# Another written order of matmuls in the attention quads that also hold an output piece

## The chip, the cores and the metric

One core of a Trainium2 chip runs the whole program. The metric is device time in microseconds of one execution. Engines are named as in the profile: PE is TensorE (PEld its weight loads), DVE VectorE, ACT ScalarE, POOL GpSimd, and SP the engine that issues nearly all DMAs.

## What is computed

A block of attention with one key and value head for 32 query heads, and a two-layer GELU network, each behind layer norms and scaled by rows made from a condition vector `c`. There are 2048 tokens of 576 numbers, heads of 18, and 4608 hidden numbers. The core of the reference:

```
mod = (silu(c) @ w_mod).reshape(6, 576)          # sa, ca, ga, sb, cb, gb
h = layernorm(x) * (1 + ca) + sa
q = (h @ wq) in 32 heads of 18;  k = h @ wk;  v = h @ wv
p = softmax(q k^T * 18 ** -0.5)                  # over 2048 keys, for each head
x = x + ga * (concat over heads (p v) @ wo)
h = layernorm(x) * (1 + cb) + sb
x = x + gb * (gelu(layernorm(h) @ w1 + b1) @ w2 + b2)
```

## The kernel before

**Stages.** The first makes keys, values and queries. The second is the attention, about 1230 us of the span, and the change lies in it. The third is the two-layer network.

**Quads.** The attention goes over 32 quads: a block of 512 tokens (`tb`, four of them) and four heads (`qd`, eight of them). A quad has, for 16 chunks of 128 keys (`kc`):

- Scores, `st_mm` (line 927): 64 matmuls of 64 x 128 by 64 x 512 (line 931) into psB banks. ACT takes the exp of each into a tile P (line 933). P has four buffers, each with four exps.
- Products, `pv_mm` (line 914): P times V (line 921), four matmuls side by side in columns, into the one psC bank. They run eight groups (`LAG`) behind the exps, that is two tiles P.
- Maxima for the next quad (some units for the one after), `mx_mm` (line 937): 48 score matmuls (line 319) into psM banks, each reduced by DVE (line 953). For eight units one more pair is folded: an X matmul (line 941, psB) is copied by ACT with a Relu into one of two buffers `xc` (line 944), and the R matmul (line 319, psM) is then reduced with it by DVE's custom operation (line 951).
- F1 and F2: `smax_fin1` reduces the maxima of quad n+1 to a column (lines 352 and 353, DVE, tile `mxf`), `smax_fin2` transposes it on PE (line 357, psB), negates it on ACT (line 359) and splits off its remainder on DVE (line 360). Four DMAs (line 364) write it as rows into the query tile QST of quad n+1, whose scores can't start before.
- The end of the quad before, `post_quad` (line 733): ACT copies psC to O when its last product is done (line 738). T1 transposes O on DVE (line 741), RC takes the reciprocal (line 744) and has POOL scale (line 745), T2 transposes back (line 747), OS copies on ACT (line 757) and subtracts on POOL (line 758), and four DMAs store the pair.
- Between tiles, `between` (line 955) lets other work step on: query loads, the second layer norm, and the weight preparation on POOL.

Score and maximum matmuls use half of PE's rows each: group 0 the lower 64, group 1 the upper.

**Buffers.** psB has four banks, psM three, psC one. A matmul that takes a bank waits until the engine that reads that bank has read its use before.

**The written order.** Engines work in order, so the order in which the program emits instructions is the order of each engine. The loop from line 980 reads it from a list of tokens, one list for each kind of quad. `S0` and `S1` are the next score of group 0 or 1, `M0`, `M1` the next maximum matmul, `X1`, `R1` the folded pair, `V4`, `V3`, `V2` as many quarters of 128 columns of the next products, `WO` an output piece, and the rest as above. `QUAD` (line 884) serves quads 0 to 8. `QUADW` (line 889) serves quads 9 to 30 and holds one `WO`, 64 `S`, 48 `M`, 8 `X1`, 8 `R1` and V tokens of 64 quarters in all; quad 31 has a list of its own.

**The output piece.** `wo_next` (line 970) takes half a tile's columns of the output product: 14 matmuls into one psB bank (line 723) and an addition on DVE (line 727). In the quads where a tile of the second layer norm is ready for it, five transposes (line 155) follow at once, in two psB banks, copied by ACT (line 165) and DVE (line 167). The same norm has its statistics on DVE (lines 143, 147, 148), which step on in `between`, at the end of every second tile of products. They come to a pattern of two quads: quads with one parity (here called even) hold statistics near F1 and the transposes at WO, the odd ones statistics near T1 and T2. From quad 27 on there are none.

Of the kernel before, what the change touches and what calls it, by code (L numbers as in the profile page):

```python
# [32 lines left out]
def block_kernel(ctx: ExitStack, tc, x, wqkv, wo, w1, b1, w2, b2, c, wmod, ident_in, out):  # L33
# [460 lines left out]
    WO, YR, ATT, B2 = {}, {}, {}, {}  # L494
# [374 lines left out]
    def tail_parts(o, tail, d, e=po):  # L869

        e.tensor_tensor(d, tail[:, 0], tail[:, 1], op=ALU.subtract)
        for x, y in ((o[:, :2], tail), (o[:, 2], d)):
# [13 lines left out]
            M1 V3 M0 S1 S1 M0 S0 R1 S0 V3 R1 S0 S1 M1 S0 M0 X1 V3 M0 S1 M0 S1 S0 S0 R1 V3 M0 X1 S0 M1 S0 M1  # L886
            V3 S1 M0 M0 S1 T2 S0 S1 V4 M0 S1 S0 M1 S0 M1 V3 S0 R1 S1 M0 F1 S1 S0 V3 X1 M0 S1 M0 R1 S0 F2 OS
            V4 M0 M1 S0 S1 M0 X1 V4 S1 M0 S1 S0 M1 M0 S1 V2 R1 S0 M1 S0 V2 S0 S1 M0 M1 V2 S1""".split()
    QUADW = """S0 M1 S0 S1 M0 S1 V4 M0 S1 M0 S1 S0 M1 V4 X1 M0 M1 S0 T1 X1 S0 V4 S0 M1 M0 S1 M0 S1 V4 S1 S0 RC
            R1 M0 S1 S0 R1 V4 S1 M0 S1 S0 M0 X1 M0 V3 S0 M1 S1 M0 S1 M0 S1 V3 S0 M1 S0 X1 M0 T2 OS V2 M0 R1  # L890
            S0 S1 S0 M1 WO X1 M0 S1 M0 R1 S0 V4 S1 M0 S1 M0 S1 M0 S1 V3 M1 S0 S0 M1 S0 S1 M0 V3 S0 M1 R1 S0
            S1 M0 V3 S0 M1 M1 S0 X1 S0 V3 M1 M0 S0 S1 R1 S0 V4 M0 S1 M0 F1 S0 S1 M0 S1 V4 F2 S1 M0 X1 M0 S1
            M0 V2 S1 S0 M1 S0 V2 M1 S0 S1 M0 V2 M0 S1 M0 S1 S1 S0 M1 V3 M0 X1 S0 R1 S0 R1 V3""".split()
    LASTW = "S0 S1 S0 S1 S0 S1 WO V4 S0 S1 V4".split()
    LAST = "S0 S1 S0 S1 V4 S0 S1 S0 S1 V4".split()
    P, PVt = {}, {}
# [83 lines left out]
    for n in range(NQT):  # L980
        ns = [0, 0]
        if n < NQT - 1:
            order = QUADW if n > NQ else QUAD
            if n == NQT - 2:
# [520 lines left out]
```

## Time and profile before

| what | value |
|---|---|
| median of 3 runs | 2234.67 us (2234.5 to 2235.53) |
| profiled execution | 2233.75 us |
| its span, first to last instruction | 2232.0 us |
| mean granted clock of PE | 0.998 |
| attention, quads 0 to 31 | about 128 to 1360 us of the span |
| quads 9 to 30 (`QUADW`) | about 469 to 1344 us |

Rows of the timeline begin with the start and the duration of a group of instructions, then the engine, the line, the operation, its output and inputs, and how many there are. A bracket behind them tells how long the engine stood idle before the group and what released it. Starts can be compared between engines. PE's matmuls are pipelined and their ends are modelled, so on PE the reader should take differences of starts, not durations. A row of the waits names the waiting engine, tile and line, what it waited for, and then the total in us, the times and the longest. A row of the windows gives the bounds of a stretch and its length, then the busy time and instructions of PE, PEld, DVE, ACT and POOL, the granted clock, the DMA share and GB/s.

### The profile page before, as it was taken

What the parts mean: (1) busy time and instruction counts of PE and PEld (TensorE: products, weight loads), DVE (VectorE), ACT (ScalarE), POOL (GpSimd) and SP (SyncE); (2) the same over time, 40 slices, a digit from 0 to 9 for tenths busy, and PEclk for the clock granted to TensorE, in tenths of its full rate; (3) what the DMA queues carried; (4) which work ended last, traced back from release to release, by engine and by line L of the source; (5) the groups of instructions that cost most, each with busy time, mean ns of one, the idle gap of its engine ahead of it and who ended that gap; (6) DMA issues with size and microseconds to landing.
All of it is one profiled execution on the core that took longest, in us unless ns stands there. A gap on an engine that the chain in (4) does not pass through costs nothing.

```text
span 2232.0 us, 45861 instructions
## 1 busy us (share of the span) xinstructions
PE 2206.7 (99%) x16454; PEld 1437.8 (64%) x16454; DVE 1936.0 (87%) x3415; ACT 1645.7 (74%) x3145; POOL 1529.3 (69%) x1761
## 2 busy tenths in 40 slices
PE   7999999999999999999999999999999999999999
PEld 5654444444444445444454445888888898988898
DVE  7589999999999999999999982887888878888887
ACT  5579999999999999999999997444444544343443
POOL 6653456777877787778776200888888867877776
PEclk9999999999999999999999999999999999999999
DMA  6232143443433333333333101655665646676563
GB/s 232 84 129 92 34 138 121 150 135 116 145 118 123 124 135 112 124 132 121 129 124 128 44 13 60 200 179 176 180 179 175 189 126 182 182 216 189 177 185 123
DMA packets 184776, 307.99 MB, mean 138 GB/s; under 512 B 19711, under 2 KB 75407, under 8 KB 184549
## 3 DMA queue, kind: packets, MB, share of 16 engines
q1 hardware_dynamic: 184405, 304.91, 43.0%
q8 instruction: 130, 2.13, 0.4%
q14 instruction: 97, 0.79, 0.1%
q10 hardware_dynamic: 144, 0.15, 0.0%
HBM read 200.97 MB, written 93.79 MB: 132 GB/s over the span
## 4 chain that ended last, share of the span: by engine, by line
PE 88%; DVE 3%; ACT 3%; issue 1%; POOL 0%; ACTq 0%; POOLq 0%; DVEq 0%
PE psC L921 22%; PE psB L1144 18%; PE psA L1247 16%; PE psB L931 14%; PE psM L319 11%; PE psB L723 2%; ACT P L933 2%; PE psB L941 2%; PE psA L1281 1%; DVE mx L953 1%; PE psA L723 1%; DVE xc L951 1%; PE psB L155 0%; PE psB L357 0%; PE psB L248 0%
## 5 line engine op out<-in xcount | busy, mean ns | idle before, releaser
L933 ACT ACTIVATE P<-psB 128x512 f32<-128x512 f32 x2008 | 1043.6, 617 | 32.3 <-PE psM L319 10.4
L953 DVE TENSOR_REDUCE mx<-psM 128x1 f32<-128x512 f32 x1476 | 938.2, 683 | 36.2 <-PE psM L319 16.5
L319 PE MATMUL psM<-KS,qst 64*128 64x512 f32 x1722 | 601.8, 442 | 0.3 <-DVE mx L337 0.2
L931 PE MATMUL psB<-qst,KS 64*128 64x512 f32 x2008 | 586.0, 430 | 0.3 <-ACT P L933 0.2
L921 PE MATMUL psC<-P,V 128*32 128x256 f32 (+3 forms) x6424 | 575.8, 448 | 0.5 <-ACT O L738 0.5
L931 PEld LDWEIGHTS psB<-qst,KS 64*128 64x128 f32 x2008 | 303.9, 185 | 216.0 <-ACT P L933 140.4
L1144 PE MATMUL psB<-ops,w1a 128*128 128x512 f32 x1512 | 393.9, 396 | 0.2 <-DVE h L1159 0.2
L319 PEld LDWEIGHTS psM<-KS,qst 64*128 64x128 f32 x1722 | 275.6, 184 | 163.2 <-DVE mx L953 121.3
L1144 PEld LDWEIGHTS psB<-ops,w1a 128*128 128x128 f32 x1512 | 270.2, 188 | 46.8 <-DVE h L1159 0.6
L921 PEld LDWEIGHTS psC<-P,V 128*32 128x32 f32 x6424 | 140.2, 108 | 200.5 <-issue 173.3
L1253 DVE TENSOR_TENSOR XT<-psA,XT 128x576 f32<-128x576 f32 x330 | 241.8, 753 | 18.5 <-PE psA L1247 13.2
L1247 PEld LDWEIGHTS psA<-w2s,big 128*128 128x128 f32 x1584 | 223.0, 188 | 14.0 <-POOL big L1221 2.5
L1247 PE MATMUL psA<-w2s,big 128*128 128x288 f32 x1584 | 230.5, 294 | 0.0
L1157 ACT ACTIVATE psB<-gs 128x512 f32<-128x512 f32 x144 | 86.7, 602 | 127.8 <-DVE gs L1156 127.8
L1221 POOL TENSOR_TENSOR big<-s,big 128x512 fp32r<-128x512 f32 x132 | 171.1, 1296 | 10.6
L1153 ACT ACTIVATE h<-psB,b1t 128x512 f32<-128x512 f32 x144 | 98.1, 681 | 102.4 <-PE psB L1144 81.4
L951 DVE CUSTOM_DVE_ANT_0 xc<-psM,xc 128x512 f32<-128x512 f32 x246 | 165.9, 681 | 4.2 <-PE psM L319 1.9
L758 POOL TENSOR_TENSOR os<-O,os 128x512 fp32r<-128x512 f32 x31 | 40.0, 1289 | 172.2 <-ACT os L757 172.2
L944 ACT ACTIVATE xc<-psB 128x512 f32<-128x512 f32 x246 | 152.4, 620 | 5.1 <-PE psM L319 2.7
L1156 DVE SCALAR_TENSOR_TENSOR gs<-psB,h 128x512 f32<-128x512 f32 x144 | 98.6, 684 | 39.9 <-ACT psB L1154 39.8
L792 POOL TENSOR_TENSOR r<-r,r 128x256 fp32r<-128x256 f32 (+1 forms) x162 | 122.1, 754 | 13.0
L1162 ACT ACTIVATE big<-h 128x512 fp32r<-128x512 f32 x39 | 24.7, 634 | 133.8 <-DVE h L1159 133.8
(212 smaller groups left out, 3326.7 us busy)
## 6 DMA issues: line engine op xcount, KB each, us to landing
w1a<-w1scr SPq DMA_DIRECT2D x252, 256.0 KB
w2s<-w2sum SPq DMA_DIRECT2D x132, 288.0 KB
w1scr<-r SPq DMA_DIRECT2D x126, 256.0 KB
w2s<-w2scr SPq DMA_DIRECT2D x76, 288.0 KB
w2scr<-r SPq DMA_DIRECT2D x72, 288.0 KB
w2sum<-r SPq DMA_DIRECT2D x72, 288.0 KB
qst<-qscr SPq DMA_DIRECT2D x192, 72.0 KB
w1a<-w2scr SPq DMA_DIRECT2D x33, 288.0 KB
```

The source lines that it names most:

```text
L319: pe.matmul(o, QST[n][64 * g:64 * g + 64, p, 128 * qt:128 * (qt + 1)], KS[64 * g:64 * g + 64, 512 * kb:512 * (kb + 1)], start=True, stop=True)
L792: po.tensor_tensor(o[:, n:2 * n], src, o[:, :n].bitcast(F32), op=ALU.subtract)
L921: pe.matmul(PVt[n][32 * j:32 * (j + 1), cs], V[:, kc, :], t[:, j, cs], start=(kc == 0 and h0 == 0), stop=(kc == 15), skip_group_check=True)
L931: pe.matmul(t, KS[64 * g:64 * g + 64, 128 * kc:128 * (kc + 1)], QST[n][64 * g:64 * g + 64, i, :], start=True, stop=True)
L933: ac.activation(P[n, kc][:, 2 * i + g, :], t, AF.Exp, scale=SCALE)
L944: ac.activation(XC[-1], t, AF.Relu)
L951: ve.tensor_tensor_reduce(c, t, c, 1.0, -3.0e38, ALU.add, ALU.max, o)
L953: ve.tensor_reduce(o, t, axis=AX.X, op=ALU.max)
L1144: pe.matmul(o, x, y, start=(first and i == 0), stop=(i == len(terms) - 1), skip_group_check=True)
L1221: po.tensor_tensor(unit(u, 1), x, unit(u, 0).bitcast(F32), op=ALU.subtract)
L1247: pe.matmul(p[:, i, :288], x[:, ts_], W2S[k][:, y], start=(bool(first) and q == 0), stop=(q == 2), skip_group_check=True)
L1253: ve.tensor_tensor(o, p[:, :, :288], o, op=ALU.add)
```

## The change

The list `QUADW` is written anew. Nothing else differs. The new list has the same tokens but for the V tokens: 20 before (eight V4, eight V3, four V2), 19 now (nine V4, eight V3, two V2).

```diff
-    QUADW = """S0 M1 S0 S1 M0 S1 V4 M0 S1 M0 S1 S0 M1 V4 X1 M0 M1 S0 T1 X1 S0 V4 S0 M1 M0 S1 M0 S1 V4 S1 S0 RC
-            R1 M0 S1 S0 R1 V4 S1 M0 S1 S0 M0 X1 M0 V3 S0 M1 S1 M0 S1 M0 S1 V3 S0 M1 S0 X1 M0 T2 OS V2 M0 R1
-            S0 S1 S0 M1 WO X1 M0 S1 M0 R1 S0 V4 S1 M0 S1 M0 S1 M0 S1 V3 M1 S0 S0 M1 S0 S1 M0 V3 S0 M1 R1 S0
-            S1 M0 V3 S0 M1 M1 S0 X1 S0 V3 M1 M0 S0 S1 R1 S0 V4 M0 S1 M0 F1 S0 S1 M0 S1 V4 F2 S1 M0 X1 M0 S1
-            M0 V2 S1 S0 M1 S0 V2 M1 S0 S1 M0 V2 M0 S1 M0 S1 S1 S0 M1 V3 M0 X1 S0 R1 S0 R1 V3""".split()
+    QUADW = """M1 M1 S0 S0 X1 S1 M0 V4 S1 M0 S1 S0 M1 M0 V4 M0 S1 S0 M0 S1 T1 M0 X1 V4 S1 RC S0 S0 M1 M0 S1 V4
+            S0 R1 M1 S0 S1 M0 S1 V3 S1 M0 S0 X1 M0 M0 S1 V2 M0 S1 S0 R1 V2 M0 X1 M0 S1 S0 S1 M0 V4 S0 T2 R1
+            M0 S1 OS S0 M1 WO S0 R1 M1 S0 M1 S0 X1 V3 S0 M1 M0 S1 S1 M1 S0 V3 M0 S1 S0 R1 S0 M0 X1 V3 M0 S1
+            X1 M0 S1 M0 S1 V4 S1 M0 R1 S0 M1 S0 V4 S0 M1 M0 F1 S1 S0 S1 V4 M0 S1 M0 X1 S0 M1 F2 V4 M1 S0 S0
+            S1 M0 S1 M0 V3 R1 S0 S0 S1 R1 M0 V3 S0 S1 M0 S1 M0 S1 V3 M0 S1 M1 S0 M1 S0 V3""".split()
```

Three places show what moves on the engines. The first is PE at F2. The rows of before run from the V4 ahead of F2 to the next products:

```order
L921 MATMUL psC<-P,V 32x512 x4
L357 MATMUL psB<-ident,mxf 16x128
L931 MATMUL psB<-qst,KS 128x512
L319 MATMUL psM<-KS,qst 128x512
L941 MATMUL psB<-KD_82,qst 128x512
L319 MATMUL psM<-KS,qst 128x512
```

The rows of the changed kernel, from the same products on:

```order
L921 MATMUL psC<-P,V 32x512 x4
L319 MATMUL psM<-KS,qst 128x512
L931 MATMUL psB<-qst,KS 128x512
L319 MATMUL psM<-KS,qst 128x512
L941 MATMUL psB<-KD_82,qst 128x512
L931 MATMUL psB<-qst,KS 128x512
L319 MATMUL psM<-KS,qst 128x512
L357 MATMUL psB<-ident,mxf 16x128
```

The transposition moved from the head of a run to its end, behind six matmuls.

The second place is DVE at F1 and F2 in an even quad (`bst` and `mv` belong to the norm's statistics). Before:

```order
L147 BN_STATS bst<-XT 128x6
L148 BN_AGGR mv_10303<-bst 128x2
L953 TENSOR_REDUCE mx_9716<-psM 128x1 x2
L352 TENSOR_REDUCE mxf<-mx_9716 128x8
L353 TENSOR_REDUCE mxf<-mx_9716 128x8
L953 TENSOR_REDUCE mx_10347<-psM 128x1
L360 SCALAR_TENSOR_TENSOR ms<-psB,ms 16x128
```

And in the changed kernel:

```order
L953 TENSOR_REDUCE mx_9766<-psM 128x1 x3
L352 TENSOR_REDUCE mxf<-mx_9766 128x8
L353 TENSOR_REDUCE mxf<-mx_9766 128x8
L147 BN_STATS bst<-XT 128x6
L148 BN_AGGR mv_10342<-bst 128x2
L953 TENSOR_REDUCE mx_10405<-psM 128x1 x3
L360 SCALAR_TENSOR_TENSOR ms<-psB,ms 16x128
```

The statistics moved behind F1's two reductions, and three maxima instead of one stand between F1 and line 360.

The third place is DVE around T2 (line 747) in an odd quad. Before:

```order
L147 BN_STATS bst<-Z_10451 128x6
L148 BN_AGGR mv_10663<-bst 128x2
L953 TENSOR_REDUCE mx_10347<-psM 128x1 x2
L747 STREAM_TRANSPOSE O<-T 128x512
L953 TENSOR_REDUCE mx_10347<-psM 128x1
L951 ISA xc,mx_10347<-psM,xc 128x512
L951 ISA mx_10347 128x1
L953 TENSOR_REDUCE mx_10347<-psM 128x1
L727 TENSOR_TENSOR XT<-psB,XT 128x288
```

And in the changed kernel:

```order
L953 TENSOR_REDUCE mx_10405<-psM 128x1 x3
L147 BN_STATS bst<-Z_10492 128x6
L148 BN_AGGR mv_10697<-bst 128x2
L747 STREAM_TRANSPOSE O<-T 128x512
L951 ISA xc,mx_10405<-psM,xc 128x512
L951 ISA mx_10405 128x1
L953 TENSOR_REDUCE mx_10405<-psM 128x1 x2
L727 TENSOR_TENSOR XT<-psB,XT 128x288
```

The statistics now stand directly ahead of T2, and the two maxima that stood between are ahead of them. ACT's copy OS came directly behind T2 in the list and now has R1, M0 and S1 between.

## Prediction

> **What bounds the kernel now.** I read the busy shares first, then one 50 us stretch of the attention, then the timeline of single quads.
>
> ```profile
> PE 2206.7 (99%) x16454; PEld 1437.8 (64%) x16454; DVE 1936.0 (87%) x3415; ACT 1645.7 (74%) x3145; POOL 1529.3 (69%) x1761
> 970.00:1020.00 50.00, 49.52 (x433) 23.92 (x430) 47.56 (x95) 47.64 (x96) 35.54 (x51) 1.00 0.39 131
> ```
>
> In a stretch of the changed quads PE, DVE and ACT all look full (49.5, 47.6 and 47.6 of 50 us), at full granted clock. The shares can't say which of the three sets the pace, so I price one quad on each. The transposition of the maxima (line 357) comes once a quad and gives the quad's length: first and last of 21, from quad 9 to quad 29, make (1295.8 - 499.8) / 20 = **39.80 us**.
>
> ```profile
> L357 PE MATMUL psB<-ident,mxf x21: 269/269/270, 499.8 to 1295.8; 128*16 128x128 f32 x21
> ACT yr L165 <- PE psB L155: 2.9, 8, 0.4
> ```
>
> PE's price comes from the timeline, from start to start, where no wait is shown. I call the matmuls between two V tokens a run. Inside a run a matmul of group 0 (S0, M0) and one of group 1 (S1, M1, R1, X1) go side by side: a slot.
>
> ```profile
> 782.08 0.64 PE L921 MATMUL psC<-P,V 128*32 128x256 f32 x8
> 782.65 0.49 PE L319 MATMUL psM<-KS,qst 64*128 64x512 f32 x1
> ...
> 783.31 0.64 PE L921 MATMUL psC<-P,V 128*32 128x256 f32 x8
> ```
>
> A V2 and a run of two slots are above, a V4 and a run of three below.
>
> ```profile
> 788.46 1.07 PE L921 MATMUL psC<-P,V 128*32 128x512 f32 x8
> 789.46 0.50 PE L319 MATMUL psM<-KS,qst 64*128 64x512 f32 x1
> ...
> 790.36 1.06 PE L921 MATMUL psC<-P,V 128*32 128x512 f32 x8
> ```
>
> V2 takes 782.65 - 782.08 = 0.57, V4 takes 1.00: about 0.2125 a quarter and 0.14 fixed. The run of two slots takes 0.66, that of three 0.90: about 0.23 a slot and 0.20 fixed. So a product block with its run costs 0.34 beside its contents. QUADW before has 20 V tokens and 68 slots (counted in order, a slot closing where the same group comes again), 64 quarters in all: 20 x 0.34 + 64 x 0.2125 + 68 x 0.23 = 36.04. WO adds 2.05 and one more restart of 0.20, F2 0.20 (rows below): **38.49 us**. Eight of the 20 (the row of L165) also hold five transposes of a norm tile, 765.93 - 765.29 = 0.64 each time, 0.26 on the mean. That leaves 39.80 - 38.75 = 1.05 us a quad in which PE waits.
>
> ```profile
> L933 ACT ACTIVATE P<-psB 128x512 f32<-128x512 f32 x2008 | 1043.6, 617 | 32.3 <-PE psM L319 10.4
> L953 DVE TENSOR_REDUCE mx<-psM 128x1 f32<-128x512 f32 x1476 | 938.2, 683 | 36.2 <-PE psM L319 16.5
> 720.03 3.04 ACT L933 ACTIVATE P<-psB 128x512 f32<-128x512 f32 x6
> 740.41 2.46 DVE L953 TENSOR_REDUCE mx<-psM 128x1 f32<-128x512 f32 x4
> ```
>
> One exp lasts 0.617, but six in a queue take 3.04: one starts every (3.04 - 0.617) / 5 = 0.48. Maxima start every (2.46 - 0.683) / 3, about 0.60. ACT needs 72 x 0.48 = 34.6 and DVE 56 x 0.60 = 33.6 a quad, each with 2 to 3 us of single operations such as the 0.63 of L757 and the 0.70 of L747 below (estimates). Both stay 2 us or more under PE's 38.5: PE is the bound, and what its order costs is paid in full.
>
> By the Trainium skill ("Perfetto Trace Analysis", Identifying the Most-Contended Engine) occupancy is the fair measure for Vector and Scalar, while Tensor is to be judged by MFU and the LDWEIGHTS share. By that rule DVE and ACT at 95% would lead and PE, with loads in 48% of the stretch, would have room, so that a block less on PE would bring nothing. Here the shares of DVE and ACT count instructions as they stand queued (0.62 long, 0.48 apart), and the bill in slots disagrees with the rule; it stays as a rival.
>
> **The change, part by part.** *Blocks and slots.* QUADW now has 19 V tokens (nine V4, eight V3, two V2; still 64 quarters) and 69 slots: one block less, 0.34, one slot more, 0.23. The bill is 38.38, or -0.11 a quad. QUADW serves quads 9 to 30, 22 of them: **-2.4 us**. The numbers of exps, maxima, copies and DMAs don't change.
>
> *The maxima's transposition, F2.*
>
> ```profile
> 738.44 1.07 PE L921 MATMUL psC<-P,V 128*32 128x512 f32 x8
> 739.60 0.27 PE L357 MATMUL psB<-ident,mxf 128*16 128x128 f32 x1
> 739.80 0.50 PE L319 MATMUL psM<-KS,qst 64*128 64x512 f32 x1
> ```
>
> That is a plain quad; below is one with norm statistics, on PE and then on DVE.
>
> ```profile
> 777.17 0.50 PE L319 MATMUL psM<-KS,qst 64*128 64x512 f32 x1
> 778.30 1.06 PE L921 MATMUL psC<-P,V 128*32 128x512 f32 x8
> 779.75 0.27 PE L357 MATMUL psB<-ident,mxf 128*16 128x128 f32 x1 [0.39 <-DVE mxf L353]
> ```
>
> On DVE:
>
> ```profile
> 777.45 0.46 DVE L147 BATCH_NORM_STATS2 bst<-XT 128x6 f32<-128x288 f32 x1
> 779.44 0.17 DVE L353 TENSOR_REDUCE mxf<-mx 128x8 f32<-128x24 f32 x1
> ```
>
> Before, F2 stands right behind a V4 (1.00) and starts 1.16 after it in a plain quad and 1.45 in one where norm statistics (L147, L148, about 0.6) stand ahead of F1 on DVE: waits of 0.16 and 0.45. From the opening of F1's run to F2 there lie 1.12 + 1.00 = 2.12 us before and 0.89 + 1.00 + 0.89 = 2.78 now, and by the order L147 and L148 stand behind F1. F1's result is there 779.61 - 777.17 = 2.44 after its run opens even with the statistics (1.85 to 2.1 without). I cost the wait at nothing: 14 x 0.16 + 8 x 0.45 = **-5.8 us**. The cover is the run that now lies ahead of F2; without it the wait is back.
>
> What that adds: L360, which gives F2's psB bank back, stands behind two statistics and three maxima (0.6 + 3 x 0.60 = 2.4 after F1) where it stood behind one maximum. The fourth psB user after F2, an S1, comes 0.2 + 1.00 + 0.57 later. In the eight quads with statistics I count 0.2 of waiting: **+1.6 us** (between 0 and 0.6, the length of the statistics). Behind that S1 two maxima and a V3 wait on PE, none on ACT. The copies of the maxima into QST come later as well.
>
> ```profile
> 780.35 2.85 SPq L364 DMA_DIRECT2D qst<-ms  x4
> 787.57 0.49 PE L931 MATMUL psB<-qst,KS 64*128 64x512 f32 x1
> ```
>
> Their issue ends at 783.20, 4.4 us ahead of the next quad's first score at 787.57. L360 about a microsecond later leaves over 3 us, and prep's stores skip two tiles ahead of F2 as before. Nothing is charged. POOL's scaling between RC and T2 gets some 8.5 us instead of 6.5 (counted by the prices above), so POOL is asked no sooner.
>
> *Output piece, T2 and OS.* An odd quad, all engines in order of time:
>
> ```profile
> 721.87 0.45 DVE L147 BATCH_NORM_STATS2 bst<-Z 128x6 f32<-128x288 f32 x1
> 722.85 0.81 PE L319 MATMUL psM<-KS,qst 64*128 64x512 f32 x2
> 723.63 0.70 DVE L747 STREAM_TRANSPOSE O<-T 128x512 f32<-128x512 f32 x1
> 724.20 2.13 PE L723 MATMUL psB<-wos,big 126*128 126x288 f32 x14
> 724.37 0.63 ACT L757 ACTIVATE os<-O 128x512 fp32r<-128x512 f32 x1 [0.80 <-DVE O L747]
> 726.25 0.50 PE L941 MATMUL psB<-KD,qst 64*128 64x512 f32 x1
> ```
>
> And an even one:
>
> ```profile
> 762.42 0.50 PE L319 MATMUL psM<-KS,qst 64*128 64x512 f32 x2
> 763.30 2.15 PE L723 MATMUL psB<-wos,big 126*128 126x288 f32 x14
> 763.48 0.63 ACT L757 ACTIVATE os<-O 128x512 fp32r<-128x512 f32 x1 [0.35 <-DVE O L747]
> 765.29 0.71 PE L155 MATMUL psB<-ident,Z 128*128 128x128 f32 x5
> 765.93 0.50 PE L941 MATMUL psB<-KD,qst 64*128 64x512 f32 x1
> ```
>
> OS directly behind T2 makes ACT stand for DVE's transpose: 0.35 in even quads, 0.80 in odd ones, where L147 and L148 delay it. PE's run ahead of WO takes 763.30 - 762.42 = 0.88 there and 724.20 - 722.85 = 1.35 here: 0.47 lost in eight quads, none where ACT stood 0.35. WO itself is 726.25 - 724.20 = 2.05. Now a V4 (1.00) stands ahead of T2, in which DVE works off its maxima, and S0, R1, M0, S1 between. In odd quads the statistics still precede T2, whose result I put 1.35 after that V4 (0.1 of backlog, 0.6, 0.65); ACT comes to OS after S0 and S1 at about 1.4. So the stall falls under 0.35: 8 x 0.47 = **-3.8 us**. If DVE is a maximum (0.60) further behind, it stays. What the wait moves: only S0 stands between OS and WO on ACT, and nobody on PE waits for os in this quad. ACT may idle over a microsecond in WO, which its slack of 2 us covers.
>
> *Quad 11.* DVE waited once for POOL there, behind a T2 that came early:
>
> ```profile
> DVE O L747 <- POOL T L745: 1.2, 1, 1.2
> ```
>
> With more room between RC and T2 half of it goes: **-0.6 us** (0 to 1.2).
>
> **Sum:** -2.4 - 5.8 + 1.6 - 3.8 - 0.6 = **-11.0 us**, 0.50 a quad, from 39.80 to 39.30. The profiled execution had 2233.75 us (span 2232.0 with 1.75 around it), which gives 2222.75; the median of the runs is 0.92 above it, so 2234.67 - 11.0 = **2223.7 us**. Stages two without QUADW and three keep their rows.
>
> *What the trace can't show:* whether the other 0.5 us a quad (1.05 less the mean of the waits priced: 0.26 at F2, 0.17 at OS, 0.05 in quad 11) stays. The new order could drop it all (22 x 0.5 = -11, to 2213) or put a stall like OS's 0.47 into every quad (+10.3, to 2234). I take no change, since both orders are runs of six or seven with at most three maxima.
>
> **Rivals.** *Slower: the xc buffers.* "S0 R1 V2 M0 X1" is new. X1's copy on ACT writes one of two xc buffers and must wait until the R1 of an earlier unit has been read by DVE. From R1's matmul to X1's lie 0.32 + 0.57 = 0.89 us, where R1 needs 0.60 on DVE behind one of 0.60 and its backlog; the old order had a V4 and most of a run, some 1.9. I count 0.3 of ACT's time. The rows of OS give the price: 0.35 of ACT's standing cost PE nothing, 0.80 cost 0.47. If DVE is two maxima further behind (1.2 more, 1.5 in all), PE loses some 1.1 a quad: 22 x 1.1 - 11.0 = +13, **2248 us**. It turns the sign from 0.85 of standing, that is a DVE one maximum late in each quad. For it: norm statistics fall into the runs before. Against: the runs ahead hold two and three maxima in 1.23 and 1.7 us, at 0.60 each no growing backlog.
>
> *No change: another engine binds,* or the waits only move: DVE's 56 maxima in bursts through three psM banks hand back half a microsecond a quad, **2234 us**, the time that the Trainium skill's rule above would also give. For it: DVE and ACT at 95%, and T1 now in a run of three maxima. Against: the bill of 38.75 of 39.80 on PE.
>
> *More:* the remaining 0.5 goes too, **2213 us**.
>
> **How the numbers follow.** Forecast 0.70, more 0.04, no change 0.12, slower 0.14. Low 2213 is the sum with every remaining wait gone, high 2234 the sum with 0.47 a quad of new waits; outside are the slower rival and a little below, under 0.2. A run of this kernel tells 0.2% (4.5 us) from no change: faster 0.74, same 0.12, slower 0.14.
>
> **What would show it.** Line 357 every 39.3 us; no wait of line 357 for mxf; ACT's wait at line 757 under 0.35; run ahead of WO at 0.89 in odd quads as in even ones; L744 to L747 with POOL out of it. I am wrong if ACT shows idle time at line 944 behind DVE's line 951, if line 931 stands behind L360, or if the quads are 39.8 long though the blocks are 19.

## The result and the profile after

| | before | after |
|---|---|---|
| median | 2234.5 us (9 runs, 2233.49 to 2235.87) | 2228.31 us (9 runs, 2227.62 to 2229.13) |
| profiled execution, span | 2233.75, 2232.0 us | 2228.3, 2226.5 us |
| quads 9 to 30, first exp to first exp | 875.5 us | 869.7 us |
| quads without norm work, with statistics at T2 (odd), with transposes (even) | 39.11, 39.60, 40.16 us | 39.27, 39.27, 39.91 us |

The changed kernel takes 0.9973 of the time before, 95% interval 0.9964 to 0.9982: **6.2 us faster**, where 11.0 were forecast. In the profiled executions, 5.5 us apart, the 22 quads take 5.8 less, and the stretch ahead of quad 9, where nothing was changed, 0.8 more. The mean granted clock is 0.998 as before.

Line 357 in the changed kernel, once a quad:

```profile
L357 PE MATMUL psB<-ident,mxf x22: 276/278/278, 500.0 to 1329.5; 128*16 128x128 f32 x22
```

(1329.5 - 500.0) / 21 = 39.50 us a quad, where 39.30 was forecast. The same 22 rows of the kernel before, with quad 30, which the prediction's 39.80 leaves out, make (1334.9 - 499.8) / 21 = 39.77. First the waits that the prediction followed. An even quad at F2, PE and then DVE:

```profile
774.54 0.49 PE L931 MATMUL psB<-qst,KS 64*128 64x512 f32 x1
...
777.33 0.28 PE L357 MATMUL psB<-ident,mxf 128*16 128x128 f32 x1
```

```profile
776.53 0.17 DVE L353 TENSOR_REDUCE mxf<-mx 128x8 f32<-128x24 f32 x1
776.62 0.45 DVE L147 BATCH_NORM_STATS2 bst<-XT 128x6 f32<-128x288 f32 x1
```

From the opening of F1's run (774.54) to F2 there are 2.79 us, and mxf is there after 776.70 - 774.54 = 2.16. F2 has 0.63 to spare and waits no more. An odd quad at T2 and WO, all engines:

```profile
721.91 0.49 PE L931 MATMUL psB<-qst,KS 64*128 64x512 f32 x1
...
722.76 0.66 DVE L747 STREAM_TRANSPOSE O<-T 128x512 f32<-128x512 f32 x1
722.80 1.88 PEld L723 LDWEIGHTS psB<-wos,big 126*128 126x128 f32 x14 [0.34 <-ACT P L933]
...
723.45 0.63 ACT L757 ACTIVATE os<-O 128x512 fp32r<-128x512 f32 x1
```

PE's run ahead of WO lasts 722.80 - 721.91 = 0.89, for 1.35 before, and ACT comes to line 757 without standing. Both waits went as forecast. Two others came that the forecast hasn't. The run with RC, "S1 RC S0 S0 M1 M0 S1", three slots, PE, its loads and ACT:

```profile
789.98 0.60 ACT L738 ACTIVATE O<-psC 128x512 f32<-128x512 f32 x1
790.47 1.57 ACT L933 ACTIVATE P<-psB 128x512 f32<-128x512 f32 x3
...
791.88 0.50 PE L931 MATMUL psB<-qst,KS 64*128 64x512 f32 x2
791.90 0.63 ACT L944 ACTIVATE xc<-psB 128x512 f32<-128x512 f32 x1
...
792.22 0.39 PE L319 MATMUL psM<-KS,qst 64*128 64x512 f32 x1
...
792.46 0.39 PE L319 MATMUL psM<-KS,qst 64*128 64x512 f32 x1
792.59 0.18 PEld L931 LDWEIGHTS psB<-qst,KS 64*128 64x128 f32 x1 [0.17 <-ACT xc L944]
...
793.01 0.16 PEld L921 LDWEIGHTS psC<-P,V 128*32 128x32 f32 x8 [0.25 <-issue]
```

The last S1 could start with the M0 at 792.46 and starts at 792.59, when ACT has copied X1 out of its psB bank (791.90 + 0.63 = 792.53). ACT is late because O's copy, 0.5 of its time, stands ahead of four psB uses. The wait is 0.13, but the run takes 793.01 - 791.88 = 1.13 and not 0.89: behind the held matmul the products come after 0.42, where the price of a run has 0.32 (0.89 less 0.34 and 0.23 to the second and third slot). So 0.24 is lost in each of the 22 quads. The first run of a quad, "M1 M1 S0 S0 X1 S1 M0", loses a little too. No copy of O stands ahead of it (that comes behind the second V4); ACT is in a row of exps:

```profile
784.29 2.79 ACT L933 ACTIVATE P<-psB 128x512 f32<-128x512 f32 x5
...
785.68 0.50 PE L319 MATMUL psM<-KS,qst 64*128 64x512 f32 x1
...
786.43 0.18 PEld L931 LDWEIGHTS psB<-qst,KS 64*128 64x128 f32 x1 [0.19 <-ACT P L933]
...
786.89 1.06 PE L921 MATMUL psC<-P,V 128*32 128x512 f32 x8
```

786.89 - 785.68 = 1.21 for four slots that cost 1.12, about 0.10 in each quad; the weights of S1 wait 0.19 for a bank that ACT's exps give back. In the waits of 520 to 1270 us, of before and then of after, it is the wait of scores (line 931) for ACT's exps that grows:

```profile
PEld psB L931 <- ACT P L933: 85.0, 149, 0.8
...
ACT os L757 <- DVE O L747: 11.5, 19, 2.1
```

```profile
PEld psB L931 <- ACT P L933: 125.6, 208, 0.8
...
PEld psB L931 <- DVE ms L360: 1.9, 8, 0.3
...
ACT os L757 <- DVE O L747: 0.5, 1, 0.5
DVE O L747 <- POOL T L745: 0.4, 1, 0.4
```

Most of these totals are weight loads that wait while PE still works; a row says where to look, and the distance of starts on PE says what it cost. With the price of a run taken off its length from start to start (medians over quads 13 to 25), the 5.8 us come out so: bill -2.4; F2 8 x 0.44 + 14 x 0.14 = -5.5; the run behind F2 in even quads 8 x 0.08 = +0.6; the run ahead of WO in odd quads 8 x 0.44 = -3.5; the run behind WO there 8 x 0.08 = +0.6; a run ahead of F1 that had lost 0.20 in even quads, -1.6; quad 11, which was 1.07 longer than the other odd quads and is 0.58 longer now, -0.5; the run with RC 22 x 0.24 = +5.2; the first run 22 x 0.10 = +2.2. Together -4.9. The rest lies in quads 9, 28 and 30, which these medians leave out, and in runs of 0.05; quad 30, in which the maxima run out, went from 40.20 to 39.37 by itself.

### The profile page after: what moved, and what is told of

It is laid out like the page before. It is cut to its first block, busy times and chain, and to the rows that moved or that the text cites. A ratio compares the mean times of both kernels' runs of the same rounds, so it can differ in the third digit from the quotient of the medians.

```text
span 2226.5 us, 46117 instructions
## 1 busy us (share of the span) xinstructions
PE 2208.1 (99%) x16630; PEld 1450.5 (65%) x16630; DVE 1932.4 (87%) x3415; ACT 1640.2 (74%) x3145; POOL 1526.5 (69%) x1761
## 3 DMA queue, kind: packets, MB, share of 16 engines
q8 instruction: 132, 2.16, 0.4%
## 4 chain that ended last, share of the span: by engine, by line
PE 91%; DVE 1%; ACT 1%; POOL 1%; issue 0%; DVEq 0%; POOLq 0%; ACTq 0%
PE psC L921 23%; PE psB L1144 18%; PE psA L1247 16%; PE psB L931 14%; PE psM L319 12%; PE psB L723 2%; PE psB L941 2%; PE psA L1281 1%; ACT P L933 1%; PE psA L723 1%; PE psB L155 0%; PE psB L248 0%; PE psB L357 0%; PE psM L931 0%; DVE mx L953 0%
## 5 line engine op out<-in xcount | busy, mean ns | idle before, releaser
L931 PE MATMUL psB<-qst,KS 64*128 64x512 f32 x2008 | 603.7, 435 | 0.1
L319 PE MATMUL psM<-KS,qst 64*128 64x512 f32 x1722 | 591.7, 435 | 0.6 <-DVE mx L337 0.5
L319 PEld LDWEIGHTS psM<-KS,qst 64*128 64x128 f32 x1722 | 284.1, 184 | 186.4 <-DVE mx L953 131.3
L921 PEld LDWEIGHTS psC<-P,V 128*32 128x32 f32 x6600 | 146.4, 108 | 185.4 <-issue 156.7
```

Source lines behind the costliest of these rows:

```text
L319: pe.matmul(o, QST[n][64 * g:64 * g + 64, p, 128 * qt:128 * (qt + 1)], KS[64 * g:64 * g + 64, 512 * kb:512 * (kb + 1)], start=True, stop=True)
L921: pe.matmul(PVt[n][32 * j:32 * (j + 1), cs], V[:, kc, :], t[:, j, cs], start=(kc == 0 and h0 == 0), stop=(kc == 15), skip_group_check=True)
L931: pe.matmul(t, KS[64 * g:64 * g + 64, 128 * kc:128 * (kc + 1)], QST[n][64 * g:64 * g + 64, i, :], start=True, stop=True)
```

## The experiments

**Theory A:** PE sets the pace; its bill is paid in full, and so is each wait for a bank, so that the two new waits for psB banks took back what the forecast lacks. **Theory B:** ACT and DVE, busy 95% of the time, set it, and a wait that is written away comes back elsewhere. All ratios are to the kernel before, with 95% intervals; a run's loss is its length less its price, as above.

### One wait of the old order at a time

e1_f2_late, in the kernel before:

```diff
-V4 F2 S1 M0 X1 M0 S1 M0 V2
+V4 S1 M0 X1 M0 S1 M0 F2 V2
```

> The order of before with one token moved: F2 goes from the head of its run to its end, behind six matmuls. Blocks, slots and everything else stay. Theory A (PE is the bound, and PE's wait for mxf ahead of line 357 is paid in full): the wait of 0.16 in 14 quads and 0.45 in 8 goes, 5.8 us, less up to 1.6 us for line 360 giving the psB bank back later: 2229 to 2231 us against 2234.5. Theory B (another engine sets the pace, PE's wait only takes up slack): 2234 to 2235 us, and the wait turns up in another run of the quad.

Measured 2234.55 us, ratio 1.0001 (0.9992 to 1.0010). F2's own wait is gone, but the run with F2 now loses 0.47 in even and 0.21 in other quads, for the 0.45 and 0.16 that F2 waited before. A plain quad, DVE and PE:

```profile
741.39 2.52 DVE L953 TENSOR_REDUCE mx<-psM 128x1 f32<-128x512 f32 x4
...
742.03 0.38 PE L931 MATMUL psB<-qst,KS 64*128 64x512 f32 x1
...
742.13 0.18 PEld L319 LDWEIGHTS psM<-KS,qst 64*128 64x128 f32 x1
...
742.56 0.28 PE L357 MATMUL psB<-ident,mxf 128*16 128x128 f32 x1
```

The M0 ahead of F2 starts 0.10 behind its partner, since DVE is late with the maxima, and F2 0.43 behind that. The wait had been DVE's lateness seen at F2; without F2 it is seen at a psM bank.

e2_os_late, also in the kernel before:

```diff
-T2 OS V2 M0 R1 S0 S1 S0 M1 WO
+T2 V2 M0 R1 S0 S1 OS S0 M1 WO
```

> The order of before with OS moved from directly behind T2 to behind the next products and two scores. Theory A: ACT's stand at line 757 shrinks from 0.80 to under 0.35 in the odd quads, and PE's run ahead of WO goes from 1.35 to 0.89 there: 8 x 0.47 = 3.8 us, 2230.5 to 2231.5 us. Theory B: ACT stands less but the quad keeps its length, 2234 to 2235 us.

Measured 2233.88, ratio 0.9999 (0.9990 to 1.0007). ACT's stand at line 757 is gone, PE's loss is not:

```profile
722.35 0.21 DVE L148 BATCH_NORM_AGGREGATE mv<-bst 128x2 f32<-128x12 f32 x1
722.48 1.24 DVE L953 TENSOR_REDUCE mx<-psM 128x1 f32<-128x512 f32 x2
...
722.86 0.81 PE L319 MATMUL psM<-KS,qst 64*128 64x512 f32 x2
...
723.77 0.18 PEld L319 LDWEIGHTS psM<-KS,qst 64*128 64x128 f32 x1 [0.30 <-DVE mx L953]
...
724.19 1.49 PEld L723 LDWEIGHTS psB<-wos,big 126*128 126x128 f32 x11 [0.24 <-issue]
...
724.71 0.63 ACT L757 ACTIVATE os<-O 128x512 fp32r<-128x512 f32 x1
```

724.19 - 722.86 = 1.33, as before. What holds PE is M1, the third psM matmul of the run: DVE has the statistics ahead of two maxima, and there are three banks. The prediction had put this loss down to ACT. In quad 11 alone the edit did gain: it falls from 40.67 to 39.93. There ACT had stood 2.1 us at line 757 (the longest of its row above), and PE had waited for the exps behind it.

e3_both has both edits.

> The order of before with both moves, F2 to the end of its run and OS behind two scores. Theory A: the two add up to 8 to 9.6 us, 2225 to 2226.5 us, which is less than the changed kernel's 2228.3 although the blocks stay 20: then the new order's own runs brought new waits. Theory B: 2234 us.

Measured 2233.86, ratio 1.0000 (0.9991 to 1.0009): nothing, as the two alone.

e4_f2_back undoes F2's place in the changed kernel:

```diff
-V4 M0 S1 M0 X1 S0 M1 F2 V4
+V4 F2 M0 S1 M0 X1 S0 M1 V4
```

> The changed order with F2 put back to the head of its run, directly behind the V4; the statistics now stand behind F1 as the V tokens set them. Theory A: a wait of about 0.16 in each of 22 quads comes back, 3.5 us, less what line 360 costs in the even ones: 2230.5 to 2232 us against 2228.3. Theory B: 2228 to 2229 us.

Measured 2236.85, ratio 1.0010 (1.0002 to 1.0019), 8.5 us over the changed kernel.

```profile
737.43 1.06 PE L921 MATMUL psC<-P,V 128*32 128x512 f32 x8
...
738.84 0.27 PE L357 MATMUL psB<-ident,mxf 128*16 128x128 f32 x1 [0.35 <-DVE mxf L353]
```

F2 comes 738.84 - 737.43 = 1.41 behind its V4, where 1.00 is free of waiting: 0.43 a quad by the medians, 22 x 0.43 = 9.4. In this order F2's late place is worth more than the 5.8 of the forecast, as F1's run is only three slots long.

### The two new waits

e5_o_on_dve takes O's copy off ACT in the changed kernel (line numbers behind it are 3 higher):

```diff
-        ac.activation(O, PV, AF.Copy)
+        if 8 <= n < 30:
+            ve.tensor_copy(O, PV)
+        else:
+            ac.activation(O, PV, AF.Copy)
```

> The changed kernel with one copy moved: in quads 8 to 29 post_quad's copy of psC to O goes on DVE instead of ACT. Theory A (PE sets the pace; the two waits that the new order brought, 0.24 a quad in the run with RC and 0.10 in the first run, come from ACT standing late behind O's copy with four psB banks): the run with RC (three slots) falls from 1.12 to 0.89, the first run stays at 1.21, and the kernel gains up to 22 x 0.24 = 5.3 us over the changed one's 2228.3, to about 2223, or to 2226 if DVE, 0.6 later by the copy, costs a psM bank somewhere. Theory B (DVE sets the pace, or the waits only move): DVE has 0.6 more in each quad, 22 x 0.6 = 13 us, and the time goes up toward 2240 while the wait in that run stays or comes back one run later.

Measured 2229.51, ratio 0.9978 (0.9969 to 0.9987): no gain over the changed kernel's 0.9973.

```profile
789.68 0.68 DVE L739 COPY O<-psC 128x512 f32<-128x512 f32 x1
...
790.42 0.16 PEld L924 LDWEIGHTS psC<-P,V 128*32 128x32 f32 x8 [0.41 <-DVE O L739]
...
791.41 0.19 PEld L934 LDWEIGHTS psB<-qst,KS 64*128 64x128 f32 x2 [0.84 <-ACT P L936]
...
792.31 0.16 PEld L924 LDWEIGHTS psC<-P,V 128*32 128x32 f32 x8 [0.24 <-issue]
...
794.11 0.18 PEld L319 LDWEIGHTS psM<-KS,qst 64*128 64x128 f32 x1 [0.27 <-DVE mx L956]
```

The run with RC is back at 792.31 - 791.41 = 0.90: the cause of the 0.24 is shown. The first run still loses 0.09, so its wait doesn't come from O's copy. But the products ahead of it now wait 0.10 for DVE to empty psC, the run behind it loses 0.10 for a psM bank (794.11), and a later run of odd quads 0.21. What ACT gave up DVE took: theory A for the wait, theory B for the sum.

e6_stats_early, in the kernel before, brings the odd quads' statistics out one run earlier:

```diff
-M0 V3 S0 M1 S1 M0 S1 M0 S1 V3 S0 M1 S0 X1 M0 T2
+M0 V4 S0 M1 S1 M0 S1 M0 S1 V2 S0 M1 S0 X1 M0 T2
```

> The kernel before with one quarter of products moved from one V token to the one ahead (V3 ... V3 to V4 ... V2), so that in odd quads the norm statistics come out one run of seven earlier, away from the maxima ahead of T2 and the output piece. Theory A (the 0.46 that odd quads lose in the run ahead of the output piece is DVE late by the statistics, with three psM banks): that run falls from 1.34 to about 0.9, eight times, and the kernel goes from 2234.3 to about 2231. Theory B (the wait moves to the run where the statistics now stand): the run ahead of the output piece is shorter, the run after the moved statistics is as much longer, 2234.3.

Measured 2234.45, ratio 0.9998 (0.9989 to 1.0007). In odd quads the run ahead of WO loses 0.28 for 0.46, the quad is 39.47 for 39.60; even quads and those without norm work are 0.05 and 0.07 longer. DVE's statistics are a part of that loss, and moving them alone is worth about nothing.

### Is a block paid in full?

e7_block_more adds a product block to the changed kernel and no work:

```diff
-V4 S1 M0 S1 S0 M1 M0 V4
+V4 S1 M0 V2 S1 S0 M1 M0 V2
```

> The changed kernel with one more product block in each QUADW quad and no other work: a V4 is written as two V2 around the run's second slot, the slots stay 69. Theory A (PE sets the pace and a block costs 0.34 whatever stands beside it): 22 x 0.34 = 7.5 us over the changed kernel's 2228.3, about 2235.8, and 0.34 on each distance of line 357. Theory B (ACT or DVE sets the pace): their work is the same, so 2228 to 2230.

Measured 2237.10, ratio 1.0011 (1.0002 to 1.0020): 8.8 us over the changed kernel, 0.40 a quad.

```profile
L357 PE MATMUL psB<-ident,mxf x22: 276/277/278, 500.5 to 1338.6; 128*16 128x128 f32 x22
```

(1338.6 - 500.5) / 21 = 39.91, 0.41 more. The block is paid in full and a little over. By runs, the two V2 and the two parts of the split run take their prices; the little over is waits that moved: the run with T1 loses 0.19 that it didn't lose, the run with RC 0.12 instead of 0.23. The 0.41 speaks against the rule of the Trainium skill that the prediction weighed ("Perfetto Trace Analysis", Identifying the Most-Contended Engine): with Vector and Scalar at 95%, more work on PE alone still costs its whole price.

### Other orders

e8_fewer_waits has the bill of the kernel before and an order meant to be free of bank waits:

```diff
+S1 S1 M1 S0 M1 S0 V4 X1 M0 S0 R1 M0 S1 V4 M0 S1 M1 S0 S1 X1 M0 T1 V3 M1 S0 S1 M0 S0 M0 S1 V3 S0 S1
+S1 M0 V2 S1 RC M0 R1 S0 S1 M0 V3 M0 S1 V1 S0 M1 S1 S0 M0 X1 V4 S1 S0 T2 M1 M0 M1 OS S0 WO M0 X1 M0
+S1 S0 M1 V3 S1 S0 S0 R1 R1 S0 V3 S1 M0 M0 X1 M1 S0 V3 M0 S1 S1 S0 M0 M0 S1 V3 M1 S0 S0 S0 M1 M0 S1
+V3 M0 R1 X1 S0 S1 X1 M0 V4 S0 R1 M0 S1 S0 M1 V4 S1 M0 S1 S0 S1 F1 M0 V4 S1 M0 S0 R1 S0 M1 F2 V4 M1
+S0 M0 S1 S0 M1 V3 M0 S1 S1 M0 S0 M0 X1 V3 R1 S0 S1 S1 M0 S0 M1 V3 M0
```

> A third order for QUADW, with the bill of the kernel before (20 blocks, 68 slots, 38.49 and 0.26 for the transposes) and not that of the changed kernel (19 and 69), but written so that by the traces no run asks for a psB or psM bank earlier than ACT or DVE give it back: F1 a run of three slots ahead of F2, O's copy ahead of a run with three psB uses in place of four, the statistics of odd quads ahead of single maxima. Theory A (what the order is worth lies in the waits): quads of 38.8 to 39.0 on the mean, so 22 x 0.5 to 0.7 under the changed kernel's 39.5, 2213 to 2217 us. Theory B (the number of blocks is what counts, or ACT or DVE binds and waits only move): 2228 to 2235.

Measured 2254.89, ratio 1.0089 (1.0075 to 1.0103): 27 us over the changed kernel, far from both theories. Most quads are 40.15 (even) and 39.46 (all others) long, for 40.16 and, with and without statistics, 39.60 and 39.11 before: its runs lose 0.20, 0.11 and four times about 0.10 a quad for banks where none had been expected, which is theory B's outcome. And four quads are 3 to 6 us longer than their neighbours. Quad 15, POOL, DVE and PE:

```profile
729.57 1.05 POOL L745 TENSOR_TENSOR T<-T,R 128x512 f32<-128x512 f32 x1
...
730.65 0.71 DVE L747 STREAM_TRANSPOSE O<-T 128x512 f32<-128x512 f32 x1 [3.67 <-POOL T L745]
...
732.00 0.54 PE L319 MATMUL psM<-KS,qst 64*128 64x512 f32 x1 [2.59 <-DVE mx L953]
```

T2 stands only eight quarters behind RC; POOL, busy with weight preparation, scales late, DVE stands for it, and PE for DVE. The windows around it (bounds, length, PE, PEld, DVE, ACT, POOL, granted clock, DMA share, GB/s) show the rest:

```profile
730.00:732.00 2.00, 0.00 (x2) 0.01 (x2) 1.35 (x3) 0.60 (x2) 1.85 (x4) 1.00 0.43 150
732.00:734.00 2.00, 1.95 (x10) 1.05 (x14) 2.00 (x4) 1.66 (x5) 1.92 (x4) 0.58 0.20 79
734.00:736.00 2.00, 2.00 (x12) 0.66 (x14) 1.29 (x3) 0.54 (x2) 1.92 (x4) 0.50 0.18 68
736.00:738.00 2.00, 2.00 (x22) 0.87 (x18) 1.25 (x4) 1.82 (x4) 1.92 (x3) 0.50 0.00 0
738.00:739.50 1.50, 1.50 (x11) 0.78 (x6) 0.34 (x3) 0.55 (x2) 1.40 (x3) 0.62 0.30 72
739.50:741.00 1.50, 1.50 (x23) 0.90 (x21) 1.50 (x3) 1.32 (x4) 1.50 (x1) 1.00 0.35 83
```

After the 2.59 us in which PE stood, it ran at half the clock for some 6.8 us, which costs about 3.3 more: the quad is 45.36 long, its like 39.46. The other three long quads look alike: PE stood 1.90, 3.27 and 3.24 us for DVE, and each time some 3.4 us at a granted clock of 0.50 followed.

e9_t2_late moves T2 and OS of e8 one and two runs back:

```diff
-V4 S1 S0 T2 M1 M0 M1 OS S0 WO M0 X1 M0 S1 S0 M1 V3 S1 S0 S0 R1 R1 S0 V3 S1 M0 M0 X1 M1 S0 V3
+V4 S1 S0 M1 M0 M1 S0 WO M0 X1 M0 S1 S0 M1 V3 T2 S1 S0 S0 R1 R1 S0 V3 S1 OS M0 M0 X1 M1 S0 V3
```

> The third order again (e8_fewer_waits), with T2 and OS written one run of products further back: 11 quarters of products and the output piece lie between RC and T2, where 8 and no output piece lay. In e8 four quads (11, 15, 19, 23) were 3 to 6 us longer than their neighbours, 19.8 us together, and in quad 15 DVE stood 3.67 us at T2 for POOL's scaling. Theory A (that stand, and what PE lost behind it, is all of the 20 us): the four quads get the length of their neighbours, 2254.9 - 19.8 = 2235, and then the third order is no faster than the kernel before, its 20 blocks having waits of their own. Theory B (the long quads come from the weight preparation or the clock, wherever T2 stands): they stay, 2250 to 2255.

Measured 2243.90, ratio 1.0036 (1.0022 to 1.0050). Quads 15, 19 and 23 are as long as their like, so the stand at T2 was the cause there (quads 10 and 11 are still 1.1 and 1.5 longer in the profiled execution, which is itself 4 us over the median; there PE stood 1.19 us for a DMA into QST, and 3.4 us at a granted clock of 0.50 followed). But T2 has come ahead of two R1, and the run behind OS waits for DVE in every quad, 0.43 where e8 lost 0.10, 22 x 0.33 = 7.3 us:

```profile
734.66 0.70 DVE L747 STREAM_TRANSPOSE O<-T 128x512 f32<-128x512 f32 x1
...
736.61 0.18 PEld L319 LDWEIGHTS psM<-KS,qst 64*128 64x128 f32 x1 [0.42 <-DVE mx L951]
```

Three more orders try bill against waits. e10_new_order:

```diff
+S1 M0 S0 M1 S1 M1 S0 V4 S1 M0 X1 S0 M1 M0 V4 M0 S1 M1 S0 S0 S1 M0 V4 S0 S1 T1 R1 S0 M1 M0 V2 X1 S0
+S1 M0 RC V3 S1 M0 S1 M0 S1 S1 M0 V4 S1 M0 X1 M0 S0 S0 R1 V3 M0 S1 S0 S1 R1 S1 M0 V4 T2 M1 S0 S0 M1
+OS M0 S1 WO M0 X1 S1 M1 S0 S0 R1 V3 S0 M1 S0 X1 M0 S0 M1 V4 S1 M0 X1 S0 M1 M0 S0 V3 S1 M0 S1 M0 S1
+S1 M0 V4 S0 R1 S0 X1 M0 R1 V3 M0 S1 S0 S1 M1 S0 F1 V4 S1 M0 M1 S0 S1 M0 F2 V4 S0 R1 X1 S1 M0 S0 M1
+V3 S1 M0 M0 S1 S0 S0 M1 V4 S1 M0 S1 S0 R1 M0 V2 S1 M0 S0 S0 M1 V2
```

> A fourth order for QUADW: 19 blocks and 70 slots, a bill of 38.61, that is 0.23 a quad more than the changed kernel's 38.38. It is written against the waits that the runs showed: the psB uses behind O's copy are spread (no five in three slots), T1 has a V4 more ahead of it, 14 quarters lie between RC and T2, F1 closes a run and a run of three slots lies ahead of F2. Theory A (what the changed kernel still loses are waits for psB and psM, 0.89 a quad without and 1.53 with the transposes, and they can be written away): quads of 39.0 to 39.2 on the mean, 22 x 0.35 = 7 to 10 us under the changed kernel's 2228.3, 2218 to 2222. Theory B (with ACT and DVE at 95% a wait that is written away comes back in another run, and only the bill counts): 22 x 0.23 = 5 us over it, 2233.

e11_low_bill:

```diff
+M1 S0 S1 M0 X1 M0 V4 M1 S0 M1 S0 M0 S1 S1 M0 S1 V4 M0 S1 S1 M0 R1 S0 S1 V4 T1 S0 M1 X1 M0 R1 S0 RC
+V3 S0 S1 S0 M1 V3 S1 M0 S0 M0 M1 S0 X1 V3 M0 S1 S0 R1 S1 S1 M0 V4 X1 M0 S0 R1 S1 M0 V2 S0 X1 M0 S1
+S1 M0 V3 M1 T2 S0 S1 M0 M0 S1 WO S0 M1 M0 M1 S0 S1 V3 S0 M1 S0 X1 M0 M0 S1 V3 M0 S1 S0 M1 S0 S0 R1
+V4 S1 M0 M0 X1 S0 M1 V3 R1 S0 M0 S1 S1 F1 S0 V3 S1 M0 M0 S1 S1 M0 V4 F2 S0 M1 M1 S0 S1 M0 V4 OS S1
+S0 M1 S0 S0 M1 V3 S1 M0 M0 S1 S1 M0 V3 S0 R1 X1 M0 S0 S0 R1 V4 S1
```

> A fifth order: 19 blocks and 68 slots, a bill of 38.15, that is 0.23 a quad less than the changed kernel's, with O's copy and T1 a run later, OS far behind T2, F2 two runs of three slots behind F1's. Theory A (bill and waits add up, and its waits are no more than the changed kernel's): at least 22 x 0.23 = 5 us under 2228.3, 2218 to 2223. Theory B (the denser a quad is on PE, the more it waits for ACT and DVE, which need the same as ever): 2227 to 2230.

e12_spread:

```diff
+M0 X1 S0 S1 R1 M1 S0 V4 S1 M0 S0 M1 M0 S1 V4 S1 M0 S0 M1 S0 S1 V4 T1 S1 M0 S0 M1 RC M1 S0 V2 S1 S0
+M0 M0 X1 V3 S1 M0 S0 M0 S1 S1 M0 V3 M0 S1 X1 M0 S0 S0 R1 V3 M0 S1 R1 S0 S1 X1 M0 V4 T2 S0 OS X1 M1
+M0 M1 S0 WO M0 S1 R1 S1 S0 S0 R1 V4 S1 M0 S0 S1 M1 X1 M0 V3 R1 S0 S1 M0 S1 S1 M0 V4 M0 X1 S0 S0 M1
+M0 S1 V4 M0 S1 S0 M1 S0 M1 V4 S0 M1 S1 S0 S1 M0 F1 V4 S1 M0 M0 S1 S0 M1 F2 V3 X1 M0 S0 M0 S1 S1 M0
+V3 S0 M1 S1 M0 S0 S0 R1 V3 S1 M0 S0 M1 V2 S0 R1 S0 S1 M1 S1 M0 V3
```

> A sixth order for QUADW with the bill of e10_new_order (19 blocks, 70 slots, 38.61) and the waits of all runs so far in view: O's copy has a run of three slots with three psB uses behind it and T1 comes at the head of the next run, T2 follows RC by 15 quarters, the statistics of odd quads fall ahead of a run with one maximum. In e10 the waits were 0.60 a quad without norm work, 0.95 in odd and 1.33 in even quads. Theory A (bill and waits simply add, and waits can be written away): 0.3 to 0.5 in plain and odd quads and 1.0 to 1.2 in even ones, so quads of about 39.2 on the mean, 22 x 0.3 = 7 us under the changed kernel's 2228.3, about 2221. Theory B (ACT and DVE at 95% leave some 0.6 to 0.9 of waiting in any order): 2228 to 2231.

Quad length less bill gives what a quad waits (even quads hold the transposes' 0.64 too):

| order | blocks, slots | bill | over it: no norm work, odd, even | time | ratio |
|---|---|---|---|---|---|
| before | 20, 68 | 38.49 | 0.62, 1.11, 1.67 | 2234.5 | 1 |
| after | 19, 69 | 38.38 | 0.89, 0.89, 1.53 | 2228.3 | 0.9973 (0.9964 to 0.9982) |
| e7_block_more | 20, 69 | 38.72 | 0.95, 1.01, 1.62 | 2237.1 | 1.0011 (1.0002 to 1.0020) |
| e10_new_order | 19, 70 | 38.61 | 0.60, 0.95, 1.33 | 2230.4 | 0.9980 (0.9971 to 0.9989) |
| e11_low_bill | 19, 68 | 38.15 | 1.30, 1.27, 1.92 | 2232.6 | 0.9990 (0.9981 to 0.9998) |
| e12_spread | 19, 70 | 38.61 | 0.64, 0.73, 1.36 | 2228.6 | 0.9975 (0.9966 to 0.9984) |

Line 357 gives the same lengths on the mean. In e10 (1332.1 - 500.4) / 21 = 39.60:

```profile
L357 PE MATMUL psB<-ident,mxf x22: 276/277/279, 500.4 to 1332.1; 128*16 128x128 f32 x22
```

In e11 39.67:

```profile
L357 PE MATMUL psB<-ident,mxf x22: 277/278/278, 502.3 to 1335.4; 128*16 128x128 f32 x22
```

In e12 39.55:

```profile
L357 PE MATMUL psB<-ident,mxf x22: 277/278/278, 499.3 to 1329.9; 128*16 128x128 f32 x22
```

The waits of the table are what the bill leaves over, so the two add up by construction; about 0.15 of each is only the products' price, which is short by up to 0.01 a token. What the table shows is that bill and waits trade: 0.23 more of bill lost 0.25 to 0.29 of waiting in quads without norm work, and 0.23 less brought 0.41 more. No order beat the changed kernel; e12 equals it. That is the part of theory B that holds: PE pays its bill in full, and yet no order got under 0.6 a quad of waiting. Whether one of 38.4 and 0.6 exists stays open.

## Why the prediction was right, and where it was not

*Bounds and bill.* That work added to PE alone is paid is shown by e7 (0.40 a quad for a block priced at 0.34). The reverse doesn't hold: e11 has 0.23 less on PE and lost more than that in waits. ACT's slack was also read too wide: 34.6 and 2 to 3 us are 0.9 to 1.9 under 38.5, and not 2 or more. The 2.4 us of the bill can't be measured by themselves.

*F2.* Right in mechanism and size: 5.5 us for the 5.8 forecast, and e4 brings the wait back. The cover named (the run ahead of F2) was the right one. That the edit alone does nothing in the old order (e1) shows that the gain needed DVE in time as well. In even quads the new order puts the statistics behind F1; what else keeps DVE in time, in quads without statistics too, no run separates.

*Line 360's bank.* Eight waits as forecast (the row of L360 above), 0.08 each for 0.2: +0.6 for +1.6.

*Output piece, T2 and OS.* The size came close, 3.5 for 3.8 us, by luck, since the cause was wrong; 0.6 of it comes back in the run behind WO, where X1's weights wait 0.18 for the bank that WO's addition on DVE (line 727) gives back late. ACT did stand at OS, as the prediction says; the step that failed is that this stand cost PE the 0.47. e2 took the stand away and left the loss: it was M1's wait for a psM bank behind DVE's statistics and two maxima. Only in quad 11, where ACT stood 2.1 us, did its stand cost PE. By e6 the place of the statistics is a part of it. That the new order cured it because DVE works off the maxima ahead of the statistics in a V4 is read from the order and not tested alone.

*Quad 11.* 0.5 for 0.6; DVE stands for POOL at line 747 once, for 0.4. e8 shows how steep this term is: with T2 eight quarters behind RC, where the kernel before has ten and the changed one fifteen, the same stand costs up to 6 us.

*The waits that stay.* This step failed: "I take no change". The prediction reasoned from the length of runs and the number of maxima, and so only from DVE and psM. It didn't add up psB uses against ACT: the two runs behind O's copy hold eight now (S1, S0, S1, X1 and S1, S0, S0, S1) and held seven. e5 shows that the copy is the cause of the larger wait; the 0.10 of the first run, which lies ahead of the copy, is only read from its row. The two cost 5.2 + 2.2 = 7.4 us; a wait gone in even quads (1.6) and less at line 360 (1.0) gave some back. With WO 0.9 and F2 0.3 short, 11.0 becomes 4.9 by these terms; of the 5.8 that the 22 quads gained, 0.9 is not priced, about what quad 30 gained beyond the others.

*Rivals.* xc: ACT stands 0.11 to 0.13 at line 944 in every quad, well under the 0.85 of the turning point, and the run that holds the late X1 loses 0.04 at most. Another engine binds: false for the sign, partly true for the size, as the table shows.

## What to carry to other kernels

Where engines share a few banks in order, price an order in two columns: the bill of the bounding engine, and for each bank pool the uses in each stretch against what its reader can give back there, with every other operation of that reader counted in. Then look for the reader that is late, not for the instruction that shows the wait: an edit that removes the place of a wait (e1, e2) or hands the work to another nearly full engine (e5) moves it. A wait of a tenth is worth writing away only if the order doesn't pay for it with a block or a slot.

## What the runs showed of the hardware

The last matmul of a run, held up for a bank by 0.1 us, costs about 0.1 more behind it: in the run with RC the next products come 0.42 after it instead of 0.32, so that a wait of 0.13 cost 0.24, and in e1 F2 comes 0.43 after the M0 that was held for 0.10.

In e8 the granted clock fell to 0.50 after PE had stood 2.59 us in quad 15 and stayed there for some 6.8 us, so the stop cost more than twice its length. After stops of 1.90, 3.27 and 3.24 us, in quads 11, 19 and 23, it stayed there for some 3.4 us. By the Trainium skill ("TensorE: Matmul & The Clock Gate", The HAM clock gate) the clock is halved after an idle window of about 3.4 us and restored after a busy one. Here stops shorter than that were enough in all four quads, and the return took about one such window three times and two once; why it took two in quad 15 no run shows.
